# First batch's sketches by rows, features from PSUM on VectorE, and the last group expert by expert in a sketched-attention and expert-attention kernel

## The chip, the cores and the metric

The kernel runs on one core of a Trainium2 chip. The metric is the device time of one execution in microseconds (us), as the median of several runs; lower is better. The engines are TensorE (PE in the profile; PEld is its weight load, which overlaps its matmuls), VectorE (DVE), ScalarE (ACT), GpSimd (POOL) and SyncE (SP), which here only issues transfers. SBUF is the on-chip memory, PSUM the accumulators that matmuls write.

## What is computed

The sizes are B=4 batches, H=4 heads, S=1088 rows, D=32, r=8. The first stage is attention through polynomial sketches, the second a mixture of four attention experts of which each row uses two:

```python
def phi(x):                              # 64 features of a row and head
    a = np.einsum('rd,bhsd->bhsr', S1, x)
    b = np.einsum('rd,bhsd->bhsr', S2, x)
    return np.einsum('bhsi,bhsj->bhsij', a, b).reshape(*x.shape[:-1], r * r)
q_p, k_p = (phi(q), phi(k))
kv = np.einsum('bhsf,bhsd->bhfd', k_p, v)
z = np.sum(k_p, axis=2)
x = np.einsum('bhsf,bhfd->bhsd', q_p, kv) / (np.einsum('bhsf,bhf->bhs', q_p, z)[..., None] + 1e-06)
# (B,H,S,D) -> (B,S,128)
logits = x @ w_gate                      # 4 experts, the 2 largest are kept
w = softmax(the two kept logits)
for e in range(4):
    scores = (x @ wq[e]) @ (x @ wk[e]).T / 8      # causal
    a = softmax(scores)
    out += w_e * ((a @ (x @ wv[e])) @ wo[e])      # w_e is 0 where e isn't kept
```

S1 and S2 come as float64 and are turned into two float32 parts, a high and a low one, by integer work on VectorE ("decode").

## The kernel before, in words

**An order by hand.** The program is a list of numbered jobs (class `Plan`). A job names its engine, or two that could do it, the values that it reads and makes and the buffers that it holds. `ORDER` (L21 to L69) is a list of job numbers; a letter behind a number says which of the two engines takes the job. The jobs are issued in that order, so it fixes the order of the instructions in the queue of each engine; nothing is moved later. An engine takes its instructions in this order and waits where an operand isn't there. Semaphores come from the framework. Jobs are numbered as they are made, so any change of the jobs comes with a new list. The figures in the jobs (`0.153`, `d_us(n)`) are what the maker of the list reckoned with; the program doesn't read them.

**Tiles.** There are four PSUM buffers of two banks each (`pair`). Rows go in 17 tiles of 64, and these in three groups: tiles 0 to 5, 6 to 11, 12 to 16. A score row (68 of them, 17 per batch) is one tile of queries against all keys up to it; its 128 partitions are 64 rows, each with its two chosen experts.

**The first stage, for each batch.** S1 and S2 are loaded (L233) into a buffer that was set to zero (L236) and decoded on VectorE (L302 to L317); `SK` is copied to four groups of partitions (L191). Meanwhile PE runs 8 matmuls of zeros to warm up (L247). k and q are loaded (L423 to L462) and transposed in blocks of 32 on VectorE (`turn k`, `turn q`, L482 to L494). The sketches (L518) are matmuls of 32x32 tiles, 32x288 each: 32 for a tensor and half of the decoded table, once with the high and once with the low part. Their results lie by columns and VectorE transposes them back out of PSUM, two of 128x576 for each of k and q (`back`, L522). Features (L527) are the products of a and b, one of 128x576 per head: those of the first batch by VectorE but for a few on POOL, those of k of the later batches mostly by POOL. k's features are summed against v (L558; 72 matmuls of two halves). For the first batch, q's features are then transposed by PE (L592) and multiplied by the sums (numerators, L615); DVE divides (L622 to L624) and PE turns x (L630). The later batches do q with its columns transposed (L686 to L757).

**The second stage.** The gate's logits (L807), the choice of two (L832 to L848), and masks that go to device memory and back (L892, L897; `md`, `mb`). Queries (L960) are kept by a base copy (L969) and a predicated pick (L973). Each score row is then: scores (L998, PE), mask and row minimum (L1010, DVE, `take`), exponential with its sum (L1026, ACT), `guard`, adding 1e-9 to the sum (L1032 on ACT or L1034 on POOL), reciprocal (L1037, DVE), `weigh`, the product with the reciprocal and the gate (L1041, POOL), a transposition by blocks (L1046, DVE). When a group's rows are done, PE takes its weighted sums of x (L1074, the 32-row tiles `xra`, `xrb`, `xrc` of x that come back from device memory `xd`).

**The end of a group.** The sums of two experts of a row are in one PSUM tile. `keep V` copies them to `agg` (L191, ACT or DVE), `patch V` overwrites rows whose second expert is the other one (L1097, DVE), `spread V` multiplies them by the masks, two experts at a time (L1101, POOL, 128x768 in groups of 384 rows). Where the rows of a group are a multiple of 128, PE multiplies by `Mo` in 128x128 pieces (L1144), piece by piece over the four experts; ACT copies each piece or all (L191) and SP stores (L1157, L1160). The group of 320 rows goes by columns (L1124), is transposed back (L1127) and stored (L1130). In the last batch the groups come in the order second, third, first.

## Time and profile before

| | |
|---|---|
| time, median of 3 runs | 279.67 us (279.2 to 280.02) |
| the profiled execution's own time | 280.91 us |
| its span on the engines | 279.2 us |
| mean granted TensorE clock | 0.994 |
| busy share | PE 94%, PEld 70%, DVE 78%, ACT 36%, POOL 55% |
| DMA | 27.36 MB moved, mean 98 GB/s; HBM read 22.22 MB, written 4.52 MB |

How to read the rows. A line of a view of groups or of the timeline names the source line (L998 is line 998 of the kernel), the engine, the operation, the tile written and the tile or tiles read (out<-in, without buffer numbers), the shapes as partitions x elements with the type, and the count (x216). In the timeline the first two figures are the start in the span and the duration, and the bracket at the end is the idle time ahead of it with what ended it. In the groups the figures behind the bar are the summed busy time, the mean of one in ns, and the idle time of the engine just before. Matmuls are counted in pairs of records where a float32 matmul runs in two passes, so a loop of 64 shows as x128. In the chain of waits, followed back from the last instruction, each step has its start, its length and its line; "issue" is time in which an engine waited for nothing that the profile shows.

### The profile page before, as it was taken

The numbers are of one execution on the slowest core, as the hardware profiler recorded it, in microseconds if no ns is written. First come the engines' busy times: TensorE is split into PE (matmuls) and PEld (weight loads), VectorE is DVE, ScalarE is ACT, GpSimd is POOL, SyncE is SP. The second block draws the span as 40 slices with busy tenths as digits, with TensorE's granted clock in tenths as the row PEclk, the third lists the DMA queues.
The fourth block names the chain that finished last, engine by engine and source line by source line (L and its number), as shares of the span: only waits on it lengthen the run. The fifth ranks groups of instructions, "written<-read, shape, count | busy, mean of one in ns | idle before, by whom it ended". The sixth has DMA issues, their size and how long they took to land.

```text
span 279.2 us, 9471 instructions
## 1 busy us (share of the span) xinstructions
PE 263.8 (94%) x3953; PEld 194.8 (70%) x3953; DVE 218.8 (78%) x541; ACT 100.2 (36%) x272; POOL 153.3 (55%) x246
## 2 busy tenths in 40 slices
PE   5789899899999999989999999999999999999993
PEld 1478575448486796676589976756696975789973
DVE  4895998999989987998969437999898468986340
ACT  2030346254333444433462331463423335233110
POOL 6323636677789834546565458655447432544570
PEclk9979999999999999999999999999999999999999
DMA  8855749921617879243900166701403756820012
GB/s 179 139 141 102 112 124 258 153 34 24 143 32 120 166 184 180 57 102 65 198 6 4 30 150 141 162 2 38 108 2 76 130 116 133 165 56 5 2 31 52
DMA packets 85547, 27.36 MB, mean 98 GB/s; under 512 B 54080, under 2 KB 84864, under 8 KB 85504
## 3 DMA queue, kind: packets, MB, share of 16 engines
q1 hardware_dynamic: 83280, 26.47, 46.4%
q8 instruction: 31, 0.51, 0.8%
q10 hardware_dynamic: 2224, 0.28, 0.6%
q14 instruction: 12, 0.10, 0.1%
HBM read 22.22 MB, written 4.52 MB: 96 GB/s over the span
## 4 chain that ended last, share of the span: by engine, by line
PE 70%; DVE 20%; issue 5%; POOL 2%; ACT 1%; DMA 1%; DVEq 0%; POOLq 0%
PE pair L1074 24%; PE pair L998 19%; PE pair L960 9%; PE pair L1144 6%; PE pair L518 3%; PE pair L558 3%; DVE AT L1046 2%; DVE w L522 2%; DVE w L1010 2%; DVE fp L527 2%; PE pair L1124 2%; PE pair L615 1%; PE pair L592 1%; DVE in L494 1%; DVE xT L191 1%
## 5 line engine op out<-in xcount | busy, mean ns | idle before, releaser
L1041 POOL TENSOR_SCALAR w<-w,rs,sh 128x384 f32<-128x384 f32 (+15 forms) x68 | 55.6, 824 | 54.8 <-DVE rs L1037 52.0
L998 PE MATMUL pair<-xT,qs 128*128 128x384 f32 (+11 forms) x216 | 76.8, 482 | 1.7 <-DVE agg L191 1.3
L1026 ACT ACTIVATE w<-w,mx 128x640 f32<-128x640 f32 (+15 forms) x68 | 52.4, 770 | 72.3 <-DVE mx L1010 56.6
L998 PEld LDWEIGHTS pair<-xT,qs 128*128 128x128 f32 x216 | 37.7, 190 | 26.9 <-issue 10.0
L1046 DVE STREAM_TRANSPOSE AT<-w 128x576 f32<-128x576 f32 (+13 forms) x68 | 50.6, 758 | 5.4 <-POOL w L1041 5.2
L1010 DVE CUSTOM_DVE_ANT_0 w<-pair,mask 128x768 f32<-128x768 f32 (+13 forms) x68 | 48.3, 721 | 5.4 <-PE pair L998 4.7
L1074 PEld LDWEIGHTS pair<-AT,xra 32*128 32x128 f32 x1136 | 41.6, 185 | 6.0 <-DVE mx L1010 2.6
L1074 PE MATMUL pair<-AT,xra 32*128 32x192 f32 (+5 forms) x1136 | 44.5, 303 | 0.0
L1101 POOL TENSOR_TENSOR agg<-agg,mb 128x768 f32<-128x768 f32 (+1 forms) x24 | 37.3, 1565 | 12.7 <-ACT agg L191 6.6
L960 PE MATMUL pair<-xT,Mq 128*128 128x384 f32 (+1 forms) x96 | 34.9, 478 | 0.1
L527 POOL TENSOR_TENSOR fp<-w 128x576 f32<-128x576 f32 x21 | 25.4, 1224 | 14.2 <-DVE w L522 12.5
L191 ACT COPY agg<-pair 128x384 f32<-128x384 f32 (+1 forms) x33 | 14.0, 462 | 44.2 <-PE pair L1074 37.7
L1074 PE MATMUL pair<-AT,xrb 32*128 32x160 f32 (+5 forms) x752 | 26.9, 287 | 0.3 <-issue 0.3
L1074 PEld LDWEIGHTS pair<-AT,xrb 32*128 32x128 f32 x752 | 26.1, 186 | 1.0 <-issue 1.0
L1144 PEld LDWEIGHTS pair<-Mo,agg 128*128 128x128 f32 x192 | 23.4, 192 | 4.1 <-POOL agg L1101 1.7
L1144 PE MATMUL pair<-Mo,agg 128*128 128x128 f32 x192 | 24.9, 279 | 1.0 <-POOL agg L1101 0.9
L960 PEld LDWEIGHTS pair<-xT,Mq 128*128 128x128 f32 x96 | 17.2, 190 | 11.2 <-issue 3.2
L973 DVE COPY_PREDICATED qs<-mb,pair 128x768 f32<-128x768 uint16 (+1 forms) x24 | 23.0, 960 | 2.4 <-DMA mb<-md 1.8
L191 DVE COPY agg<-pair 128x384 f32<-128x384 f32 (+1 forms) x15 | 7.9, 532 | 13.1 <-PE pair L1074 11.7
L518 PE MATMUL pair<-in,SK 32*32 32x288 f32 x416 | 13.4, 494 | 3.0 <-DVE in L494 3.0
L522 DVE STREAM_TRANSPOSE w<-pair 128x576 f32<-128x576 f32 x16 | 11.6, 756 | 5.6 <-PE pair L518 5.6
L1097 DVE COPY_PREDICATED agg<-mb,pair 128x384 f32<-128x384 uint16 (+1 forms) x24 | 12.6, 550 | 3.3 <-ACT agg L191 2.9
(160 smaller groups left out, 295.4 us busy)
## 6 DMA issues: line engine op xcount, KB each, us to landing
mb<-md SPq DMA_DIRECT2D x7, 576.0 KB, 5.2
xra<-xd SPq DMA_DIRECT2D x16, 192.0 KB, 4.3
xrb<-xd SPq DMA_DIRECT2D x16, 192.0 KB, 3.6
xrc<-xd SPq DMA_DIRECT2D x16, 160.0 KB, 4.9
mb<-md SPq DMA_DIRECT2D x4, 480.0 KB, 5.4
in<-in_k_dram SPq DMA_DIRECT2D x12, 136.0 KB, 4.1
in<-in_q_dram SPq DMA_DIRECT2D x3, 544.0 KB, 5.5
xd<-w SPq DMA_DIRECT2D x12, 136.0 KB, 3.5
```

The costliest lines, as they stand in the source:

```text
L191: (nc.scalar.copy if eng == "ACT" else VEC[eng].tensor_copy)(o, i)
L527: VEC[e].tensor_tensor(out=f, in0=a[:, :, None, R : 2 * R].to_broadcast([128, NJ, R, R]), in1=a[:, :, 0:R, None].to_broadcast([128, NJ, R, ...
L960: nc.tensor.matmul(plan[ps[x]][:, y, 0:w], Mq[:, ((1, 2), (0, 3))[x][y]], plan[xT][:, 64 * t0 : 64 * t1], start=True, stop=True)
L973: nc.vector.copy_predicated(chosen(), rows(c), rows(plan[ps[x]]))
L998: nc.tensor.matmul(plan[p][:, y, 0 : c1 - c0], plan[qs][:, 128 * t : 128 * t + 128], plan[xT][:, c0:c1], start=True, stop=True)
L1010: nc.vector.tensor_tensor_reduce(out=o, in0=src, in1=msk, scale=-1.0, scalar=mx[:, b, i, x - 1 : x] if x else 3e38, op0=ALU.add, op1=ALU.m ...
L1026: nc.scalar.activation(out=a, in_=a, func=ACTF.Exp, bias=mx[:, b, i, last : last + 1], scale=-1.0, accum_out=zs[:, b, i : i + 1])
L1041: nc.gpsimd.tensor_scalar(out=a, in0=a, scalar1=rs[:, b, i : i + 1], scalar2=plan[("sh", b)][:, i : i + 1], op0=ALU.mult, op1=ALU.mult)
L1046: nc.vector.transpose(dst[:, 0 : keys // 32, t], plan[A][:, 0:keys].rearrange("p (j s) -> p j s", s=32))
L1074: nc.tensor.matmul(plan[Vk[g // 2]][:, g % 2, lo : 32 * nt], plan[(f"xr{j // 12}", b)][rows, j % 12], a[rows, j, lo:], start=(j == 0), sto ...
L1101: nc.gpsimd.tensor_tensor(out=a, in0=a, in1=plan[mb][:, 2 * x : 2 * x + 2, 0:w], op=ALU.mult)
L1144: nc.tensor.matmul(plan[p][0:m, 0, 128 * x : 128 * x + 128], plan[agg][:, e, 128 * x : 128 * x + m], Mo[:, e], start=(e == 0), stop=(e == ...
```

## The change

- **S loads and decode.** S1 and S2 are each loaded twice, into rows 0 to 15 and 16 to 31, by the queue of SP and that of ACT; the memset of that buffer goes. The decode is in two halves, for the high part and the low part. Besides `SK` it fills block tables `SKW`, which are zero but for each head's own 16 columns.
- **k first.** The first half of the first batch's k goes out first, on ACT's queue.
- **First batch's sketches by rows.** `sketch_rows` takes 64 rows of two heads as the stationary operand and `SKW` as the moving one: 64x64 tiles, 32 columns, 144 matmuls for k and q. The results lie by rows in PSUM. ACT copies the first factor (and the fourth head's second factor) to SBUF; `head_features` multiplies: heads 0 to 2 on VectorE with the second factor read straight from PSUM, head 3 on POOL, in two parts of 4 and 5 blocks of 128 rows (k: 5 and 4). The back transpositions of this batch go. k's sums are in two parts as well, and the features' transpositions of q's first part no longer wait for the second.
- **Second batch's k by rows.** Nine matmuls of 128x128 give the high and the low part beside each other (`sketch_all`), ACT copies them out, POOL adds the two parts (four instructions) and makes the features in five pieces (`row_features`).
- **Reciprocals.** `invert` has a second engine: POOL raises to the power -1. In the new list 32 of the 68 score rows use it.
- **Last group expert by expert.** For the last group of the last batch, VectorE multiplies the first expert of each pair straight out of PSUM by its mask, ACT keeps the second, VectorE patches it and `scale_one` multiplies it by its mask. PE takes the experts in the order 0, 2, 1, 3, three pieces of 128 rows each; ACT or DVE copy each piece, and the three pieces are stored separately, one by SP and two by ACT.
- **A new list.** `ORDER` is another, for 1307 jobs instead of 1270; it also has 20 warming matmuls (18 at the start, 2 among the last group's projections) instead of 12 (8 at the start, 4 at 47 us), and other engines for some jobs. The k of batches 2 and 3 stays as it was, with two back transpositions and four features each.

```diff
--- before
+++ after
@@ ORDER @@
-56 45 47 0 1 8a 77 60 46 3 2 76 25a 19a 17a 48 79 49 51 78 57 90 89 74 87 75 88 50 13b 98 100 99 102a 103a 91 92 83 93
...
+71 0 46 45 85 5a 40b 19b 42a 29a 10a 12b 2 98 1 47 44 51 55 87 52 86 99 89 38a 15a 27a 59 30a 74 8b 88 62 60 33a 54 50
...
     def load_sketch(eng, x):
-        eng.dma_start(out=room(0, 64)[R * x : R * x + R], in_=(S1, S2)[x].bitcast(I32))
-
-    def first():
-        nc.vector.memset(room(0, 64), 0)
+        for r in (R * x, 2 * R + R * x):
+            eng.dma_start(out=room(0, 64)[r : r + R], in_=(S1, S2)[x].bitcast(I32))
...
     def make_ident():
+        nc.gpsimd.memset(SKW, 0.0)
...
+    def decode(lower):
...
+        if not lower:
+            ve.tensor_scalar(out=ex, in0=hi, scalar1=20, scalar2=0x7FF, op0=SHR, op1=AND)
+            ve.tensor_scalar(out=ma, in0=hi, scalar1=0xFFFFF, scalar2=3, op0=AND, op1=SHL)
+            ve.tensor_scalar(out=sg, in0=hi, scalar1=31, scalar2=31, op0=SHR, op1=SHL)
+            ve.tensor_scalar(out=ex, in0=ex, scalar1=896, scalar2=0, op0=ALU.subtract, op1=ALU.max)
+            ve.scalar_tensor_tensor(out=ma, in0=lo, scalar=29, in1=ma, op0=SHR, op1=OR)
+            ve.tensor_single_scalar(ex, ex, 255, op=ALU.min)
+            ve.scalar_tensor_tensor(out=sg, in0=ex, scalar=23, in1=sg, op0=SHL, op1=OR)
+            ve.tensor_tensor(out=ma, in0=ma, in1=sg, op=OR)
+            ve.scalar_tensor_tensor(out=S_hi, in0=ex, scalar=0, in1=ma.bitcast(F32), op0=ALU.is_gt, op1=ALU.mult)
+            ve.transpose(SK[0:32, 0], S_hi)
+        else:
+            ve.tensor_single_scalar(lw, lo, 0x1FFFFFFF, op=AND)
+            ve.tensor_copy(last, lw)
+            ve.scalar_tensor_tensor(out=S_lo, in0=last, scalar=2.0**-52, in1=sg.bitcast(F32), op0=ALU.mult, op1=ALU.mult)
+            ve.transpose(SK[0:32, 1], S_lo)
+    def spread_blocks(e, h, s):
+        copy(e, SKW[32 * h : 32 * h + 32, s, :, h, :], SK[0:32, s, 0 : 2 * R].rearrange("d (x r) -> d x r", x=2))
...
-            job(f"load k{b}.{x}", "SP", 0.45 if early else 0.7, lambda e, x=x: load_k(nc.sync, x), lead,
-                ("kin", b, x if early else 0), [kin], landing=1.6 if early else 0.95, rank=rank(-0.1))
+            job(f"load k{b}.{x}", ("ACT", "SP")[x] if early else "SP", 0.45 if early else 0.7,
+                lambda e, x=x: load_k(nc.scalar if e == "ACT" else nc.sync, x), lead,
...
+        def sketch_rows(nm, j0, j1, t):
+            src = plan[("in", nm + "T", b)]
+            for j in range(j0, j1):
+                for m in range(2):
+                    for half in (0, 64):
+                        rows, y = slice(64 * m, 64 * m + 64), 128 * j + half
+                        for s in range(2):
+                            nc.tensor.matmul(plan[t][half : half + 64, m, 32 * (j - j0) : 32 * (j - j0) + 32].rearrange(
+                                "p (x d) -> p x d", x=2), src[rows, y : y + 64],
+                                SKW[rows, s, :, 2 * m : 2 * m + 2].rearrange("p x h r -> p x (h r)"),
+                                start=(s == 0), stop=(s == 1))
+        def kept_first(nm, j0, j1):
+            return plan[ab[nm]][:, 4 * R * j0 : 4 * R * j1].rearrange("p (m j d) -> p m j d", m=2, d=2 * R)
+        def kept_last(nm, j0, j1):
+            return plan[ab[nm]][:, 4 * R * NJ + R * j0 : 4 * R * NJ + R * j1].rearrange("p (j r) -> p j r", r=R)
+        def in_psum(t, nj):
+            return plan[t][:, :, 0 : 4 * R * nj].rearrange("p m (j x d) -> p m j x d", x=2, d=2 * R)
+        def copy_sketch(y, nm, j0, j1, t):
+            s = in_psum(t, j1 - j0)
+            if y == 0:
+                for m in range(2):
+                    nc.scalar.copy(kept_first(nm, j0, j1)[:, m], s[:, m, :, 0])
+            else:
+                nc.scalar.copy(kept_last(nm, j0, j1), s[:, 1, :, 1, R:])
+        def head_features(e, nm, h, j0, j1, t):
+            nj = j1 - j0
+            r = slice(R * (h % 2), R * (h % 2) + R)
+            second = in_psum(t, nj)[:, h // 2, :, 1, r] if h < 3 else kept_last(nm, j0, j1)
+            f = plan[fps[nm]].rearrange("p (j h x y) -> p j h x y", h=H, x=R, y=R)[:, j0:j1, h]
+            VEC[e].tensor_tensor(out=f, in0=second[:, :, None, :].to_broadcast([128, nj, R, R]),
+                                 in1=kept_first(nm, j0, j1)[:, h // 2, :, r, None].to_broadcast([128, nj, R, R]), op=ALU.mult)
+        def sketch_all(nm, j0, j1, t):
+            src = plan[("in", nm + "T", b)]
+            for j in range(j0, j1):
+                nc.tensor.matmul(plan[t][:, (j - j0) // 4, 128 * (j % 4) : 128 * (j % 4) + 128], src[:, 128 * j : 128 * j + 128],
+                                 SKW.rearrange("p s x h r -> p (s x h r)"), start=True, stop=True)
+        def sketch_keep(nm, a, j0, j1, t):
+            src = plan[t][:, a, 0 : 128 * (j1 - j0)].rearrange("p (j y d) -> p y j d", y=4, d=4 * R)
+            nc.scalar.copy(plan[ab[nm]].rearrange("p (y j d) -> p y j d", y=4, j=NJ)[:, :, j0:j1], src)
+        def sketch_add(nm, j0, j1):
+            a = rows_ab(nm)
+            for x in range(2):
+                nc.gpsimd.tensor_tensor(out=a[:, 0, x, j0:j1], in0=a[:, 0, x, j0:j1], in1=a[:, 1, x, j0:j1], op=ALU.add)
+        def row_features(e, nm, j0, j1):
+            a = rows_ab(nm)[:, 0, :, j0:j1].rearrange("p x j (h r) -> p x (j h) r", h=H)
+            n = H * (j1 - j0)
+            f = plan[fps[nm]].rearrange("p (j h x y) -> p (j h) x y", h=H, x=R, y=R)[:, H * j0 : H * j1]
+            VEC[e].tensor_tensor(out=f, in0=a[:, 1, :, None, :].to_broadcast([128, n, R, R]),
+                                 in1=a[:, 0, :, :, None].to_broadcast([128, n, R, R]), op=ALU.mult)
...
+        tcuts = ((0, 4), (4, NJ))
+        kcuts = ((0, 5), (5, NJ))
...
+                    for h in range(H):
+                        n = R * R * nj
+                        job(f"{'phi' if h < 3 else 'features'} {nm}{b}.{h}{x}", "DVE" if h < 3 else "POOL", d_us(n) - 0.05 if h < 3 else 0.09 + 0.0019 * n,
+                            lambda e, nm=nm, h=h, j0=j0, j1=j1, t=t: head_features(e, nm, h, j0, j1, t),
+                            [("ab", nm, b, x, 0)] + ([("ab", nm, b, x, 1)] if h == 3 else []), ("fp", nm, b, x), [*([t] if h < 3 else []), ab[nm], fps[nm]], rank=at + 0.01 * h)
...
+            elif b == 1 and nm == "k":
...
-        def invert():
-            nc.vector.reciprocal(rs[:, b, i : i + 1], rs[:, b, i : i + 1])
+        def invert(e):
+            r = rs[:, b, i : i + 1]
+            if e == "DVE":
+                nc.vector.reciprocal(r, r)
+            else:
+                nc.gpsimd.tensor_tensor(out=r, in0=r, in1=minus, op=ALU.pow)
...
-        job(f"invert {b}.{i}", "DVE", 0.153, lambda e: invert(), [("zg", b, i)], ("r", b, i), rank=rank)
+        job(f"invert {b}.{i}", ("DVE", "POOL"), (0.153, 0.555), invert, [("zg", b, i)], ("r", b, i), rank=rank)
...
+        if last_group(b, n):
+            def mix(x):
+                nc.vector.tensor_tensor(out=by_half(plan[agg][:, x]), in0=sums_of(x), in1=by_half(plan[mb][:, x]), op=ALU.mult)
+            def scale_one(e, x):
+                a = plan[agg][:, 2 + x, 0:w]
+                VEC[e].tensor_tensor(out=a, in0=a, in1=plan[mb][:, 2 + x, 0:w], op=ALU.mult)
...
+            def project_expert(e, first_, last_):
+                for x in range(3):
+                    nc.tensor.matmul(piece(x), plan[agg][:, e, 128 * x : 128 * x + 128], Mo[:, e], start=first_, stop=last_)
+            def keep_piece(e, x):
+                copy(e, plan[ob][:, 128 * x : 128 * x + 128], piece(x))
+            def store_piece(e, x):
+                (nc.scalar if e == "ACT" else nc.sync).dma_start(out=out[b, 64 * t0 + 128 * x : 64 * t0 + 128 * x + 128],
+                                                                in_=plan[ob][:, 128 * x : 128 * x + 128])
+            order = (0, 2, 1, 3)
+                job(f"out {b}.{n}.{e}", "PE", 12 * 0.056, lambda _, e=e, y=y: project_expert(e, y == 0, y == 3),
...
```

## The prediction

> **What bounds the kernel now.** I read the page first, then the busy time by stage, then the timeline of the head and of the end, then the chain of waits. The page:
>
> ```profile
> PE 263.8 (94%) x3953; PEld 194.8 (70%) x3953; DVE 218.8 (78%) x541; ACT 100.2 (36%) x272; POOL 153.3 (55%) x246
> PE 70%; DVE 20%; issue 5%; POOL 2%; ACT 1%; DMA 1%; DVEq 0%; POOLq 0%
> ```
>
> TensorE looks saturated, but 94% is an average over stages. The busy time of each engine in stretches that I cut at the events named below (columns: stretch, its length, busy time of PE, PEld, DVE, ACT and POOL with instructions, granted clock, DMA share, GB/s), and of DVE alone from the first division to the last transposition ahead of the first group's sums:
>
> ```profile
> 16.30:19.80 3.50, 3.50 (x28) 3.17 (x30) 3.50 (x6) 1.44 (x4) 0.00 (x0) 0.51 0.71 191
> 23.10:62.90 39.80, 36.77 (x463) 23.39 (x459) 37.24 (x107) 16.74 (x49) 23.33 (x50) 1.00 0.71 137
> 62.90:178.00 115.10, 113.69 (x1785) 85.37 (x1784) 95.20 (x230) 43.35 (x122) 72.33 (x104) 1.00 0.51 103
> 178.00:268.90 90.90, 90.54 (x1390) 71.58 (x1390) 68.20 (x162) 34.26 (x90) 45.12 (x61) 1.00 0.34 71
> 268.90:279.20 10.30, 5.51 (x32) 4.14 (x32) 2.60 (x5) 1.34 (x3) 3.28 (x2) 1.00 0.16 35
> ...
> 24.75:60.89 36.14, 33.79 (x99) 1.00 0.76 146
> ```
>
> So there are three stages. To 23 us PE waits for the first batch's sketches and features. From 23 to 63 us DVE is busy 37.24 of 39.80 us. From 63 us on PE is busy 98.8% (113.69 of 115.10), then 99.6% (90.54 of 90.90). After 268.9 us comes a tail of 10.30 us with PE busy about half. A change pays in the first two stages and in the tail; in the third only what TensorE itself does counts. The chain of waits confirms the second stage; in its middle it runs through DVE:
>
> ```profile
> 47.54 1.50 DVE fp L527
> ...
> 49.39 1.29 DVE fp L735
> 50.68 0.93 DVE qs L973
> ```
>
> The head (start, duration, engine, line, operation, tiles, shapes, count):
>
> ```profile
> 1.31 3.59 PE L247 MATMUL pair<-idle 128*128 128x512 bf16 x8 [1.31 <-DVE idle L240]
> 3.79 0.58 DVE L302 TENSOR_SCALAR w<-w 32x32 int32<-32x32 int32 x1 [2.54 <-DMA w<-in_S_dram]
> 7.93 4.95 PE L518 MATMUL pair<-in,SK 32*32 32x288 f32 x128 [3.03 <-DVE in L494]
> 12.04 2.82 DVE L527 TENSOR_TENSOR fp<-w 128x576 f32<-128x576 f32 x2
> ...
> 16.26 2.77 DVE L527 TENSOR_TENSOR fp<-w 128x576 f32<-128x576 f32 x4
> 16.28 2.79 PE L592 MATMUL pair<-ident,fp 128*128 128x128 f32 x12 [0.23 <-DVE w L522]
> 19.00 2.62 PE L558 MATMUL pair<-vp,fp 128*64 128x33 f32 x72
> 21.55 1.60 PE L518 MATMUL pair<-in,SK 32*32 32x288 f32 x64
> 23.09 4.23 PE L615 MATMUL pair<-kvz,fp 128*128 128x66 f32 x36
> 24.75 0.17 DVE L622 TENSOR_SCALAR den<-pair 128x12 f32<-128x12 f32 x1
> 27.96 2.31 POOL L527 TENSOR_TENSOR fp<-w 128x576 f32<-128x576 f32 x2 [1.49 <-DVE den L622]
> 28.14 0.56 DVE L624 TENSOR_TENSOR w<-pair,den 128x384 f32<-128x384 f32 x1
> 30.22 1.46 POOL L370 CAST AT<-ident 64x1536 bf16<-64x1536 f32 x1
> 30.23 1.48 DVE L833 TENSOR_TENSOR ch<-ch 128x12 f32<-128x12 f32 x1
> ...
> 60.52 0.45 DVE L1046 STREAM_TRANSPOSE AT<-w 128x256 f32<-128x256 f32 x1
> 62.89 0.61 PE L1074 MATMUL pair<-AT,xra 32*128 32x192 f32 x8
> ```
>
> Two things to see. The same 64 sketch matmuls took 4.95/2 = 2.5 us at 7.93 and 1.60 us at 21.55, and the clock was granted at 0.51 from 16.3 to 19.8. And a DVE feature product took 1.41 us (2.82/2) beside POOL's, 0.69 us (2.77/4) alone, while L624, one of whose inputs is PSUM, took 0.56 us beside POOL's L527.
>
> **The change part by part.** Prices of single instructions, by shape (count, busy, mean ns, idle before), and the landing of a k load (us to landing last):
>
> ```profile
> L522 DVE STREAM_TRANSPOSE w<-pair 128x576 f32<-128x576 f32 x16 | 11.6, 756 | 5.6 <-PE pair L518 5.6
> L1037 DVE RECIPROCAL rs<-rs 128x1 f32<-128x1 f32 x68 | 8.9, 140 | 7.8 <-POOL rs L1034 5.9 <-ACT rs L1032 1.7
> L1097 DVE COPY_PREDICATED agg<-mb,pair 128x384 f32<-128x384 uint16 x16 | 8.8, 579 | 0.7 <-ACT agg L191 0.4
> ...
> L867 POOL TENSOR_TENSOR ch<-ch,c 128x44 f32<-128x44 f32 x1 | 0.7, 687 | 0.1
> L340 POOL TENSOR_TENSOR pick<-pick 128x8 f32<-128x8 f32 x1 | 0.2, 203 | 0.1
> ...
> in<-in_k_dram SPq DMA_DIRECT2D x1, 256.0 KB, 4.0
> ```
>
> *Start of the sketches.* k's first half goes first on ACT's queue, so it is in by about 0.8 + 4.0 = 4.8 us at the latest. But S1 and S2 are each loaded twice now, two issues a queue, S2 behind k; the decode, which starts at 3.79 in the old kernel, stands behind those issues and behind two transpositions of k on DVE, say at 5. From decode to sketches the old kernel took 7.93 - 3.79 = 4.1 us for 16 instructions, a copy and q's transpositions; the new one has 14, three k transpositions and four block copies, about as much. POOL's one-hot cast (1.46 us) now falls on the decode's second half; L833 waited through it. So first sketches at 8.7 to 11, taken 9.5, against 7.93: +1.6. k first buys nothing by itself.
>
> *Sketches by rows.* 144 matmuls, seen as 288, replace 128 for k and q of the first batch; tiles of 64x64 are not in the trace. Below: 4.6 us, if four tiles overlap where L558's two do not (half of 2.62/72 = 36 ns is 18; 16 ns taken). Above: 288 x 36 ns = 10.4. I take 25 ns, as L518 (1.60/64): 7.2 us, to 16.7. The old pair took 4.95. The 18 instead of 8 warming matmuls (3.59/8 = 0.45 us each) last to about 9, so the clock should be full here and in the transpositions L592, which took 2.79/12 = 0.23 us at 0.51.
>
> A rule of the Trainium skill speaks against this step: "TensorE: Matmul & The Clock Gate" (Wait — 56ns, not 53.3ns?) says that with hardware decode off the sequencer spends about 62 ns on each matmul; by it 288 of them would take 17.9 us, an estimate from the page, and the forecast would come out about 10 us later. L518's 25 ns (1.60/64) do not agree, so that floor is not in force here.
>
> *Features.* Four back transpositions of 0.756 us leave DVE (3.0). Twelve products of 256 or 320 columns read PSUM: by L624 (0.56 us for 384) 0.40 to 0.48 each, 5.3 in all, where six of 576 took 2.82 + 2.77 = 5.6. Twelve small ACT copies come ahead of them. DVE's order puts the first product of q's second part ahead of k's second part, so nearly six products follow q's last sketch: 16.7 + 0.6 + 2.6 = 19.9. Then k's sums (2.62, at most), eight transpositions (0.9 to 1.9), the second batch's sketches by nine matmuls of 128 columns (18 records at 2.50/20 = 0.125, a row of the tail below: 2.3) stand ahead of the numerators: 24.3, against 23.09. Term: **+1.2**, from -1.6 to +4.
>
> The products are priced as unhindered. The Trainium skill, "GPSIMD Engine Reference" (Specifications), names contention with DVE instructions of two SBUF inputs; the 1.41 us of two-SBUF-input products beside POOL and the 0.56 us of L624 beside it agree; were PSUM no shelter, twelve products at double price would add 5 us.
>
> *DVE from the first division to the last transposition of the first group.* 33.79 us of work in 36.14. From the order of the new instructions, with the old durations, that stretch loses two of three 576-wide products (2.05, one of them the slow one), one back transposition of the second batch's k (0.7; k's features go to POOL), a turn of q (0.6), L833's stall (1.0 with its neighbours, the one-hot cast being early), one score and one pick that now come later (1.5); a few copies come. 28.0 us remain; at the same density (93%) 30.0. That is -6.1; PE's own queue shares it, so I take **-5.5**, from -3.0 (all that PE idles in 23.1:62.9, 39.80 - 36.77) to -7.
>
> *Thirty-two of 68 reciprocals become a power on POOL.* DVE loses 32 x 0.14 = 4.5 us and waits that stood behind it; POOL gains 32 x 0.2 (L340) to 0.69 (L867), taken 0.4: 13 us. No row shows a power. In the third stage DVE has 20 us to spare to 178 us and POOL 43, so both are cover; without it, each power adds its price less 0.14 to the way exp, weigh, turn, sums. With the new order and copies moved to ACT: **-1.0**, from -4 to +5, since PE lacks only 1.8 us in that stage by the records.
>
> *Tail.* Old rows:
>
> ```profile
> 268.78 2.42 PE L1124 MATMUL pair<-agg,Mo 128*128 128x320 f32 x8
> 268.92 0.86 ACT L191 COPY agg<-pair 128x384 f32<-128x384 f32 x2 [2.66 <-PE pair L1074]
> 269.61 3.30 POOL L1101 TENSOR_TENSOR agg<-agg,mb 128x768 f32<-128x768 f32 x2 [1.88 <-ACT agg L191]
> ...
> 272.96 2.50 PE L1144 MATMUL pair<-Mo,agg 128*128 128x128 f32 x20 [0.95 <-POOL agg L1101]
> 275.54 0.48 ACT L191 COPY ob<-pair 128x384 f32<-128x384 f32 x1 [5.76 <-issue]
> 276.04 0.39 SPq L1157 DMA_DIRECT2D out_dram<-ob  x1
> ```
>
> From the last sum to the end: 10.3. New, counted from there: DVE multiplies one expert (0.58) and patches two (0.58 each) by 1.8; then its queue holds the turn of the other group's output, which waits for PE's L1124 until 2.4, and ends at 2.9; second expert 3.5, last scaling 4.1; POOL's one scaling (half of 1.65) is done long before. PE's last six matmuls end at 4.9, ACT's two copies at 5.5, its two stores are issued by 6.3 (0.39 each), and land 2.8 later as before (279.2 - 276.43): 9.1. **-1.3**, from -2.4 (no wait in DVE's queue) to -0.4.
>
> Sum: 1.2 - 5.5 - 1.0 - 1.3 = -6.6. The profiled execution took 280.91 us (span 279.2), 1.2 over the median of 279.67; I put the difference on the median: **273.1 us**.
>
> **Rivals.**
> - *Sketches eat the head.* At 36 ns, with a start at 11, the numerators begin 4 us later than now: 273.1 + 2.8 = 276. For it: 288 tiny matmuls; against: L518's 25 ns with two tiles fewer in conflict.
> - *PE is already the bound in the second stage.* Then only its 3.0 us of idle can go there, and -1.0 becomes 0: 273.1 + 2.5 + 1.0 = 276.6. For it: 36.77 of 39.80 busy; against: ends of matmuls are modelled, and the chain above runs on DVE.
> - *Slower: the power on POOL.* Place: between guard and weigh of 32 of 68 score rows, in POOL's queue, with the spreads of the sums behind it. Each costs its price less 0.14 where POOL is the late one; if that is one time in two, 6.6 us are gone at 0.14 + 6.6/16 = 0.55 us a power, and at 1.0 us it is 273.1 + 16 x 0.6 = 283. For it: no row has this operation, and L867 needs 0.69 for 44 elements; against: 0.20 for eight elements, and POOL idles 45%.
> - *More than forecast.* DVE off the path up to 178 us and a short sketch: -1.6 - 7 - 2.5 - 1.4 = -12.5: 267.
>
> **How the numbers follow.** Forecast 0.52, sketches 0.13, PE bound 0.11, power 0.15, more 0.09. About 0.3% (0.8 us) can be told from no change. Faster: 0.52 + 0.09 + 0.20 of the two middle rivals' 0.24 = 0.81; slower 0.13 + 0.02 = 0.15; same 0.04. The range 267.5 to 279.5 leaves out the slow power case (0.15) and a little below.
>
> **What would show it.** First matmul on SKW near 9.5 us and 25 ns between them; granted clock 1.00 all through 9 to 24; numerators near 24; first weighted sum near 58 instead of 62.89; POOL's power near 0.4 us; the tail 9 us with the turn of the output ahead of the second expert's product. Wrong, if the first sums start after 61, if PE idles more than 2% between them and the tail, or if powers take over 0.6 us.

## The result, and the profile after

The changed kernel takes 281.36 us (median of 17 runs, 280.08 to 288.46) against 279.90 us before (17 runs beside them): a ratio of 1.0065, 95% interval 1.0039 to 1.0091, so 1.8 us slower where 6.6 us faster was forecast. In part of the runs of most kernels with the changed head the granted clock is 0.98 or 0.97 and the time 2 to 7 us longer; the ratios leave the longest of these out. The profiled execution took 281.35 us (span 279.6).

The page of the changed kernel, busy time and the chain's shares by engine:

```profile
PE 265.6 (95%) x4074; PEld 198.4 (71%) x4075; DVE 211.2 (76%) x519; ACT 105.1 (38%) x288; POOL 169.9 (61%) x286
PE 75%; DVE 6%; DMA 6%; issue 4%; POOL 3%; ACT 2%; SPq 1%; DVEq 0%; POOLq 0%; ACTq 0%
```

DVE does 7.6 us less than before and has gone from 20% to 6% of the chain, as was meant. The time did not follow. The view by stages shows why (columns as in the prediction; the cuts are the first numerators, the first weighted sums and the end of the last ones; first the changed kernel, then the same cut of the old one):

```profile
0.00:23.34 23.34, 19.14 (x414) 13.95 (x415) 14.63 (x46) 6.23 (x22) 11.83 (x41) 1.00 0.73 147
23.34:60.78 37.44, 35.83 (x457) 23.12 (x456) 32.13 (x99) 16.39 (x50) 28.13 (x58) 1.00 0.89 154
60.78:270.05 209.27, 205.19 (x3174) 157.00 (x3173) 161.23 (x368) 81.21 (x214) 129.06 (x186) 1.00 0.43 85
270.05:279.60 9.55, 5.39 (x33) 4.31 (x34) 3.22 (x7) 1.29 (x4) 0.92 (x1) 1.00 0.19 40
```

```profile
0.00:23.09 23.09, 17.25 (x293) 10.34 (x293) 15.56 (x39) 4.46 (x9) 9.27 (x30) 0.93 0.66 139
23.09:62.90 39.81, 36.78 (x463) 23.41 (x459) 37.24 (x107) 16.74 (x49) 23.33 (x50) 1.00 0.71 137
62.90:268.90 206.00, 204.23 (x3174) 156.95 (x3174) 163.39 (x391) 77.62 (x211) 117.45 (x165) 1.00 0.43 89
```

From the numerators to the end PE is busy for 265.55 - 19.14 = 246.4 us now, and was for 263.77 - 17.25 = 246.5 (the sums of the two views less their first rows). The second stage is 2.4 us shorter, but 0.95 us of this is PE work that now stands behind the first sums, and PE's idle time there fell only from 3.03 to 1.61. In the third stage it rose from 1.77 to 4.08; three waits make 2.9 of that (0.96 us for features on POOL at 112 us, 1.26 us behind no semaphore at 150 us, 0.72 us for a copy on ACT at 170 us). The tail lost 0.75 us.

The head of the changed kernel (start, duration, engine, line, operation, tiles, shapes, count, idle before):

```profile
1.24 6.95 PE L254 MATMUL pair<-idle 128*128 128x512 bf16 x18 [1.24 <-DVE idle L243]
6.48 1.49 POOL L386 CAST AT<-ident 64x1536 bf16<-64x1536 f32 x1
6.68 1.33 DVE L324 SCALAR_TENSOR_TENSOR w<-w 32x32 f32<-32x32 f32 x1
8.12 0.30 PE L571 MATMUL pair<-SKW,in 64*64 64x32 f32 x2
9.23 0.42 PE L571 MATMUL pair<-SKW,in 64*64 64x32 f32 x6 [0.81 <-DVE SKW L193]
9.99 3.35 PE L571 MATMUL pair<-SKW,in 64*64 64x32 f32 x196 [0.34 <-ACT SKW L193]
14.45 1.58 PE L571 MATMUL pair<-SKW,in 64*64 64x32 f32 x84 [1.12 <-issue]
15.96 1.09 PE L718 MATMUL pair<-ident,fp 128*128 128x128 f32 x8
23.34 2.79 PE L741 MATMUL pair<-kvz,fp 128*128 128x66 f32 x24
```

A sketch matmul takes 3.35/196 = 17 ns, not 25. The sketches begin in earnest at 9.23 (9.5 was taken), numerators at 23.34, not 24.3. In the middle stands an idle time of 1.12 us behind no semaphore ("issue"); more on it in the last section. The decode's L324 waited through the one-hot cast, as expected.

The groups of the products and of the powers (count, busy, mean ns, idle before):

```profile
L599 DVE TENSOR_TENSOR fp<-pair,w 128x320 f32<-128x320 f32 x6 | 2.7, 484 | 2.1 <-ACT w L590 2.1
L599 DVE TENSOR_TENSOR fp<-pair,w 128x256 f32<-128x256 f32 x6 | 2.3, 414 | 0.0
...
L1167 POOL TENSOR_TENSOR rs<-rs,minus 128x1 f32<-128x1 f32 x32 | 18.0, 562 | 12.0 <-ACT rs L1158 7.8 <-DVE qs L1099 3.1
```

The products that read PSUM cost what was estimated (0.40 to 0.48). A power costs 0.562 us, not 0.4.

The tail of the changed kernel:

```profile
266.86 3.18 PE L1204 MATMUL pair<-AT,xra 32*128 32x192 f32 x92
269.97 2.42 PE L1275 MATMUL pair<-agg,Mo 128*128 128x320 f32 x8
272.22 2.84 PE L1301 MATMUL pair<-Mo,agg 128*128 128x128 f32 x24
272.43 0.52 DVE L1278 STREAM_TRANSPOSE ob<-pair 128x320 f32<-128x320 f32 x1 [0.29 <-PE pair L1275]
275.39 0.36 SPq L1307 DMA_DIRECT2D out_dram<-ob  x1
275.56 0.85 ACTq L1307 DMA_DIRECT2D out_dram<-ob  x2
```

The new projection's matmuls follow the other group's on PE without a gap, where PE waited for POOL's spreads before. The last stores are issued by 276.41, 6.4 us behind the last sum (forecast 6.3), and took 3.2 us to the end, not 2.8.

### The profile page after: what moved, and what is told of

It reads as the page before. It is cut to its first block, busy times and chain, and to the rows that moved or that the text cites. A ratio compares the mean times of both kernels' runs of the same rounds, so it can differ in the third digit from the quotient of the medians.

```text
span 279.6 us, 9762 instructions
## 1 busy us (share of the span) xinstructions
PE 265.6 (95%) x4074; PEld 198.4 (71%) x4075; DVE 211.2 (76%) x519; ACT 105.1 (38%) x288; POOL 169.9 (61%) x286
## 4 chain that ended last, share of the span: by engine, by line
PE 75%; DVE 6%; DMA 6%; issue 4%; POOL 3%; ACT 2%; SPq 1%; DVEq 0%; POOLq 0%; ACTq 0%
PE pair L1204 23%; PE pair L1124 21%; PE pair L1086 8%; PE pair L1325 6%; PE pair L677 3%; PE pair L1275 3%; PE pair L535 2%; PE pair L571 2%; DMA vp<-in_v_dram 2%; DMA xd<-w 2%; PE pair L741 1%; DMA out_dram<-ob 1%; POOL agg L1231 1%; DVE w L1136 1%; PE pair L933 1%
## 5 line engine op out<-in xcount | busy, mean ns | idle before, releaser
L1152 ACT ACTIVATE w<-w,mx 128x128 f32<-128x128 f32 (+14 forms) x68 | 52.4, 770 | 64.5 <-DVE mx L1136 52.4
L1171 POOL TENSOR_SCALAR w<-w,rs,sh 128x512 f32<-128x512 f32 (+15 forms) x68 | 55.6, 822 | 19.3 <-DVE rs L1165 15.6
L1136 DVE CUSTOM_DVE_ANT_0 w<-pair,mask 128x768 f32<-128x768 f32 (+14 forms) x68 | 48.3, 727 | 11.4 <-PE pair L1124 11.1
L1176 DVE STREAM_TRANSPOSE AT<-w 128x512 f32<-128x512 f32 (+16 forms) x68 | 50.3, 757 | 3.8 <-POOL w L1171 3.7
L1204 PE MATMUL pair<-AT,xra 32*128 32x160 f32 (+5 forms) x1136 | 44.8, 302 | 0.0
L1204 PEld LDWEIGHTS pair<-AT,xrb 32*128 32x128 f32 x752 | 26.7, 185 | 1.5 <-issue 1.5
L1167 POOL TENSOR_TENSOR rs<-rs,minus 128x1 f32<-128x1 f32 x32 | 18.0, 562 | 12.0 <-ACT rs L1158 7.8
L1325 PEld LDWEIGHTS pair<-Mo,agg 128*128 128x128 f32 x168 | 19.9, 192 | 2.2 <-issue 0.8
L1160 POOL TENSOR_SCALAR rs<-zs 128x1 f32<-128x1 f32 x29 | 7.0, 243 | 23.5 <-ACT w L1152 15.2
L1325 PE MATMUL pair<-Mo,agg 128*128 128x128 f32 x168 | 20.6, 276 | 0.0
L544 POOL TENSOR_TENSOR fp<-w 128x576 f32<-128x576 f32 x13 | 15.3, 1176 | 0.2
L193 ACT COPY qs<-pair 128x384 f32<-128x384 f32 (+1 forms) x22 | 9.4, 470 | 15.7 <-PE pair L1086 8.4
```

Source lines behind the costliest of these rows:

```text
L193: (nc.scalar.copy if eng == "ACT" else VEC[eng].tensor_copy)(o, i)
L1136: nc.vector.tensor_tensor_reduce(out=o, in0=src, in1=msk, scale=-1.0, scalar=mx[:, b, i, x - 1 : x] if x else 3e38, op0=ALU.add, op1=ALU.m ...
L1152: nc.scalar.activation(out=a, in_=a, func=ACTF.Exp, bias=mx[:, b, i, last : last + 1], scale=-1.0, accum_out=zs[:, b, i : i + 1])
L1167: nc.gpsimd.tensor_tensor(out=r, in0=r, in1=minus, op=ALU.pow)
L1171: nc.gpsimd.tensor_scalar(out=a, in0=a, scalar1=rs[:, b, i : i + 1], scalar2=plan[("sh", b)][:, i : i + 1], op0=ALU.mult, op1=ALU.mult)
L1176: nc.vector.transpose(dst[:, 0 : keys // 32, t], plan[A][:, 0:keys].rearrange("p (j s) -> p j s", s=32))
```

## The experiments

Ratios are to the kernel before on the same chip, with 95% intervals; 0.36% is 1 us. Where only the list is edited, the diff names the jobs.

### The parts alone

Powers undone in the changed kernel:

```diff
-invert 0.1@POOL ... (32 rows)
+invert 0.1@DVE ... (32 rows)
```

> The changed kernel with all 68 reciprocals on DVE again (the 32 powers on POOL took 0.562 us each, 18.0 us in all). Theory A: the powers are what gave the third stage its new idle time of PE (4.1 us from the first sums to the tail, 1.8 in the old kernel): PE's idle there falls to about 2 us, the time by 1.5 to 2.5 us against the changed kernel, to about 279. Theory B: the new order of the jobs is what made it, and the powers lie in time that POOL has to spare: idle stays at 3.5 to 4.5 us and the time within 0.7 us of the changed kernel's 281.4, more likely above it, since DVE gets 32 x 0.14 us back.

Measured: 294.54 us, 1.0516 (1.0465 to 1.0567). Neither theory: it is 13 us slower than the changed kernel, and tells of something else. The group of the reciprocals in that kernel:

```profile
L1165 DVE RECIPROCAL rs<-rs 128x1 f32<-128x1 f32 x68 | 8.9, 147 | 11.6 <-ACT rs L1158 6.8 <-POOL rs L1160 4.8
```

The instruction costs 0.147 us, but DVE now stands idle for 11.6 us ahead of these, waiting for `guard`, with minima and transpositions queued behind. The 32 places in the list suit POOL's queue and not DVE's, so the run says nothing of the power's price. The clean form is the next one, which puts the powers into the kernel before:

```diff
-invert 0.1@DVE ... (the same 32 rows)
+invert 0.1@POOL ...
```

> The kernel before with the same 32 reciprocals as powers on POOL, nothing else. Theory A: POOL gets 18 us more, sums wait for weighed rows, PE's idle time in the third stage goes from 1.8 to about 4 us: 1.5 to 2.5 us slower than before. Theory B: POOL has the room: within 0.7 us of before. My forecast took -1.0 for this step with the order and copies; by it the run is 0 to 1 us faster.

Measured: 281.47 us, 1.0043 (1.0025 to 1.0061), +1.2 us, between the theories and on the slower side. The powers' group in this kernel:

```profile
L1044 POOL TENSOR_TENSOR rs<-rs,minus 128x1 f32<-128x1 f32 x32 | 18.6, 581 | 9.7 <-ACT rs L1035 8.6
```

Each costs 0.44 us more than DVE's reciprocal (0.581 - 0.14). 1.2 us is what some three of the 32 would cost if they lay on the path to the sums (an estimate, 1.2/0.44; which of them do was not traced).

The last group, undone in the changed kernel and alone in the old one:

```diff
 def last_group(b, n):
-    return b == B - 1 and n == 0
+    return False
```

> The changed kernel with the last group's end as in the old one (four copies, two patches, two spreads on POOL, pieces one by one, one store). The tail after the last weighted sum was 10.3 us before and 9.55 after. If the tail was worth what these spans say, this is 0.75 us slower than the changed kernel with a tail of 10.3; by my forecast 1.3 slower; if the end of the changed kernel is set elsewhere (stores of the other group), no change.

Measured: 281.99 us, 1.0069 (1.0035 to 1.0103). It is slower than the changed kernel's 1.0065 by too little to be told from nothing; the intervals allow 0.75 us, and 1.3 us only just. So this run doesn't show that the new end is worth anything in the changed kernel.

```diff
+if last_group(b, n): mix, keep, patch, scale; project_expert; store_piece
```

> The kernel before with the last group's end of the changed one, nothing else. By the spans 0.75 us faster than before (tail 9.55), by my forecast 1.3 us (tail 9.0); if the gain in the changed kernel came from the other order of the last rows, about 0.

Measured: 278.97 us, 0.9950 (0.9930 to 0.9970): 1.4 us faster. The stretch behind the last sum in this kernel:

```profile
268.63:277.30 8.67, 5.03 (x33) 4.21 (x32) 3.24 (x7) 1.29 (x4) 0.92 (x1) 0.93 0.19 42
```

8.67 us, where the forecast had 9.1 and the old kernel 10.30. In the old kernel this step was right. By its ratio this kernel is the fastest of all that were run, ahead of the kernel before and of the changed one; the next ones (0.9971, 0.9977) overlap with it.

The changed head alone, with the old order from the numerators on, and then with the second batch's k by rows:

```diff
-            elif b == 1 and nm == "k":
+            elif False:
```

> The changed kernel's head alone (k first, decode in halves, first batch's sketches by rows, features from PSUM, 18 warming matmuls), then the old order to the end, the second batch's k, the reciprocals and the last group as before. By the spans of the two profiles numerators start at 23.3 instead of 23.1, and what DVE saves behind them buys nothing if PE is the bound: 0 to 0.7 us slower than before. By my forecast (+1.2 for the head, about -2 for the stall and the turn of q that go from DVE's stretch): 0.5 to 1 us faster.

Measured: 280.88 us, 1.0041 (1.0012 to 1.0070): 1.15 us slower, outside both readings. In its profile numerators begin at 25.24, 2.15 us later than before, and the stretch from there to the first sums is 38.60 us, 1.2 us shorter. In three of the twelve runs the granted clock was 0.97 or 0.982 and the time 283.0 to 284.5 us; the median of the other nine is 280.5, 0.5 us above before, so part of the 1.15 us is the clock.

> As the run with the head alone, and the second batch's k by rows too (nine matmuls of 128x128, copies on ACT, adds and five feature pieces on POOL): two back transpositions (1.4 us) and one product (1.4 us) less on DVE, about 3 us more on POOL. By my forecast about 2 us faster than the head alone; if PE is the bound, within 0.7 us of it; if POOL's pieces come late for the sums against v, up to 1.5 us slower.

Measured: 280.92 us, 1.0054 (1.0022 to 1.0087). Taking three DVE instructions of the second batch away on top of the head brings nothing that can be told from the head alone.

### What bounds the second stage

```diff
-            job(f"pick {b}.{n}.{x}", "DVE", d_us(2 * w), lambda _, x=x: pick(x),
+            job(f"pick {b}.{n}.{x}", "DVE", d_us(2 * w), lambda _, x=x: None if b == 0 else pick(x),
```

> The kernel before without the six predicated picks of the first batch (its queries stay those that the base copies wrote): DVE does about 6 x 0.97 = 5.8 us less before the first group's sums, nothing else changes for PE. If DVE bounds the second stage, as the step -5.5 of my forecast has it, the time falls by about 5 us, to 275. If PE bounds it, only PE's idle time of that stage (3.0 us) can go: 0.5 to 2.5 us faster.

Measured: 279.94 us, 1.0001 (0.9984 to 1.0017). This is the run that settles the largest term. The second and third stage of this kernel, cut at the same events as above:

```profile
22.27:62.19 39.92, 36.55 (x462) 23.38 (x457) 32.01 (x101) 16.74 (x49) 23.36 (x50) 1.00 0.74 137
62.19:267.25 205.06, 203.44 (x3174) 156.54 (x3173) 163.43 (x390) 77.61 (x211) 117.44 (x165) 1.00 0.43 89
```

DVE has 32.01 us of work where it had 37.24, and the stretch is as long as before (39.92 against 39.81), with PE at 36.55. 5.2 us of DVE are worth nothing. PE's two longest waits in this stage are the same (in us: total, times, longest), first in the kernel before, then in this one:

```profile
PE pair L906 <- DVE ch L811: 1.4, 1, 1.4
PE pair L757 <- DVE w L522: 0.9, 1, 0.9
```

```profile
PE pair L757 <- DVE w L522: 1.6, 1, 1.6
PE pair L906 <- DVE ch L811: 1.4, 1, 1.4
```

They are for two single results of DVE, the choice of experts and one back transposition, and neither wait got shorter with less work elsewhere in DVE's queue.

The opposite, more work for PE:

```diff
-dummy22@- dummy19@- dummy26@- dummy7@-
+score 0.4.00 dummy22@PE ... score 0.2.00 dummy19@PE ... query 0.2.01 dummy26@PE ... query 0.2.11 dummy7@PE
```

> The kernel before with eight more warming matmuls (0.39 us each, 3.1 us of PE) spread over 35 to 57 us, behind four jobs of scores and queries. If PE bounds the second stage: 2 to 3.1 us slower. If DVE bounds it, PE has 3.0 us to spare there and the time moves by less than 1 us.

Measured: 281.41 us, 1.0054 (1.0033 to 1.0074): +1.5 us for 3.1 us of matmuls, between the two readings. PE had room for half of them. So neither engine's busy time alone gives the length of the stage: PE's work does for the most part, with about 1.5 us of waits in it that more work can use.

### The order

```diff
 ORDER: the changed kernel's jobs (abridged)
-the changed kernel's order and engines behind the numerators
+the old kernel's order and engines behind the numerators, where it has the job
```

The list of jobs also says which engine takes a job, and some 75 jobs differ in this between the two lists (`guard`, copies and features above all). What this run tells apart is the list as a whole, not the order alone.

> All parts of the change (head, second batch's k by rows, 32 powers on POOL, last group expert by expert), but behind the numerators in the old order. The parts alone gave: head with k by rows +1.5 us (0.54%), powers +1.2, last group -1.4. If they add, this is 1.3 us slower than before, where the changed kernel is (+1.8): then the new order is worth about nothing. If the new order is what costs, this is within 0.5 us of before; if the new order makes room for the powers on POOL, this is over 2.5 us slower than before.

Measured: ratio 0.9996 (0.9963 to 1.0029); median of all runs 280.76. All parts of the change, by the old list, take what the old kernel takes. The second stage, the third and the tail of this kernel, cut at the same events:

```profile
23.07:62.31 39.24, 36.54 (x458) 23.32 (x457) 33.08 (x100) 17.84 (x54) 25.21 (x53) 1.00 0.69 134
62.31:268.63 206.32, 204.24 (x3174) 156.78 (x3173) 162.68 (x363) 77.90 (x213) 134.22 (x195) 1.00 0.43 89
268.63:277.17 8.54, 5.03 (x33) 4.21 (x32) 3.24 (x7) 1.29 (x4) 0.91 (x1) 1.00 0.19 42
```

PE idles 2.1 us in the long third stretch (206.32 - 204.24), against 4.1 in the changed kernel, although POOL has the powers here too (134.22 us). Ahead of the first sums it is the other way round: 2.70 us here, 1.61 in the changed kernel. So the new list wins 1.1 us of idle time in the second stage and loses 2.0 in the third; its tail is 1.0 us longer in these two profiles. The parts alone sum to 1.5 + 1.2 - 1.4 = 1.3 us; the interval of this run, -1.0 to +0.8, misses that, but with the parts' own intervals (together about 1.2 us either way) the two agree.

The same without the powers (68 reciprocals on DVE):

> All parts of the change but the powers (68 reciprocals on DVE), in the old order. The powers cost 1.2 us when put into the kernel before. If they cost the same here, this is 1.2 us faster than all parts in the old order, about 1.2 under before; if the head and the last group leave POOL the room, within 0.4 us of it.

Measured: 0.9977 (0.9942 to 1.0013), median 280.80. The two intervals overlap too far to say what the powers cost here.

Two picks behind three transpositions, in the changed kernel:

```diff
-pick 2.0.0@DVE pick 2.0.1@DVE weigh 1.12 turn A 1.12 ... turn A 1.14 ... turn A 1.13
+turn A 1.14 turn A 1.13 weigh 1.12 turn A 1.12 pick 2.0.0@DVE pick 2.0.1@DVE
```

> The changed kernel with two picks of the third batch put behind three transpositions (turn A) in DVE's order. In the changed kernel they waited 1.0 us for a mask fetch at 146.7 us, with the transpositions behind them, and PE idled 1.26 us at 149.7. If that idle time hangs on DVE's queue, it goes: 1.2 us faster than the changed kernel, and fewer runs at a low clock. The view of waits says "issue" there, that is no semaphore; if PE ran out of instructions (its last instruction packet came at 148.2 and took 1.36 us), the gap stays at 149 to 151 us and the time within 0.5 us of the changed kernel.

Measured: 281.04 us, 1.0039 (1.0007 to 1.0071). PE's gap stayed at 150.1 us with 1.00 us, so it doesn't hang on DVE's queue. The changed kernel's waits at that place:

```profile
PEld pair L1204 <- issue: 1.5, 1, 1.5
PE pair L1204 <- issue: 1.3, 1, 1.3
```

### Filling idle times of PE

In the old kernel with the new last group; then there without the move at 32 us and with a fuller one at 124 us (copies on ACT, a transposition of x later); then that one with all parts by the old list:

```diff
-widen 1@PE widen 0@PE query 0.0.00@PE
+query 0.0.00@PE widen 1@PE widen 0@PE
-choose a2.0 choose b2.0 ... patch V 1.0.0 ... patch V 1.0.1 ... keep V 1.0.1@DVE
+choose a2.0 patch V 1.0.0 patch V 1.0.1 keep V 1.0.1@DVE choose b2.0
```

> The kernel before with the changed last group and three jobs moved in the order: the first batch's second query matmul ahead of the mask matmuls that wait for the choice (PE idle 1.37 us at 32.4), and the patches and one copy of the second batch's first sums ahead of the second half of the third batch's choice on DVE (PE idle 1.32 us at 124.3, score waiting for a PSUM buffer). If PE's idle time is what counts everywhere: 1.4 (last group) + 0.9 + 1.3 = 3.6 us faster than before. If a stall filled in one place comes back in the next: 1.4 us faster, as the last group alone.

Measured: 279.78 us, 0.9997 (0.9980 to 1.0014): slower than the same kernel without the filling (0.9950). The score that waited at 124.3 starts at once, and the next pair of scores waits instead, in this kernel's timeline:

```profile
126.78 1.29 DVE L770 STREAM_TRANSPOSE w<-xT 128x1088 f32<-128x1088 f32 x1
128.23 0.73 DVE L1011 CUSTOM_DVE_ANT_0 w<-pair,mask 128x576 f32<-128x576 f32 x1
129.02 2.29 PE L999 MATMUL pair<-xT,qs 128*128 128x352 f32 x4 [1.83 <-DVE mx L1011]
```

In this profile the granted clock is 0.50 from 129.50 to 132.91, right behind that gap (more in the last section).

> The kernel before with the changed last group and the same filling (the other filling, of the idle time at 32 us, left out). If the idle time at 124 us goes without one in its place: 1.4 + 1.3 = 2.7 us faster than before, 277.3. If it comes back further on, as in the run with both fillings, 0 to 1.4 us faster.

Measured: 278.96 us, 0.9971 (0.9953 to 0.9990): no better than the last group alone; the gap stands at 127.9 with 1.59 us.

> All parts of the change in the old order, and one idle time of PE (1.32 us at 124.3, a score that waits for a PSUM buffer) filled: four copies on ACT and two patches ahead of the second half of the choice on DVE, a transposition of x behind the score's minimum. Of 12 runs without this, seven took 278.9 to 279.4 us and five 282.2 to 283.5, nearly all of those at a clock of 0.982. If idle times over about 1.3 us bring a window of 3.41 us at half clock (1.7 us), the low clocks go and the median falls from 280.8 to 278 to 278.5. If the low clocks have another cause, about half the runs stay at 282 to 283.

Measured: 279.41 us, 0.9980 (0.9963 to 0.9997), with the gap come back at 133 us in the same way. One run of twelve had a clock of 0.982 instead of five, but its profile shows the low clock in the head (last section), which the filling doesn't touch, and full clock behind the gap at 133 us: the first reading falls. That fewer runs had it is not explained by this.

### Warming

```diff
-9 jobs of two warming matmuls at the start
+4 jobs
```

The kernel before has eight at the start too; of its other four, two come at 12.8 us and two at 47.7.

> The changed kernel with 8 warming matmuls at the start instead of 18 (they end at about 4.5 us, the first sketch starts at 8.1). If the long warming is what lowers the granted clock later, the time falls by 0.5 to 1 us and the clock is above 0.985 in all runs. If it is needed for the sketches, they run at half the clock as in the old kernel (16.3 to 19.8 us) and the time rises by 1 to 3 us.

Measured: 283.50 us, 1.0119 (1.0077 to 1.0160): 2.1 us slower than the changed kernel, with clocks of 0.980 to 0.992. In its profile two stretches behind 3.41 us with PE nearly idle are at half clock, and the sketches fall into them:

```profile
5.58:8.99 3.41, 0.28 (x2) 0.19 (x2) 3.10 (x11) 0.46 (x1) 1.87 (x3) 1.00 1.17 220
8.99:12.40 3.41, 2.86 (x89) 2.75 (x91) 1.99 (x8) 1.13 (x3) 0.00 (x0) 0.50 0.46 97
12.40:15.82 3.42, 3.42 (x139) 3.42 (x137) 2.33 (x7) 0.87 (x6) 1.99 (x4) 0.50 0.81 126
```

> The kernel with the changed head alone, 8 warming matmuls instead of 18. Same two readings: 0.5 to 1 us faster than the head alone (+1.15 us against before) if the long warming lowers the clock later, 1 to 3 us slower than it if the sketches need it.

Measured: 281.05 us, 1.0026 (1.0009 to 1.0043). The shorter warming makes the changed kernel slower, and its profile shows the second reading at work; that the long warming lowers the clock later is not borne out. The head alone comes out no slower with the shorter one, and its profile has full clock in the sketches: the warming is not needed in every execution.

Ten more matmuls of zeros in the head:

```diff
+dummy, dummy ahead of sketch k0.0
             if nm == "k" and j0:
+                for _ in range(6):
+                    nc.tensor.matmul(plan[t][:, 0, 256:512], idle[:, 0:128], idle[:, 0:256], start=True, stop=True)
```

> All parts of the change but the powers, in the old order, and ten more short matmuls of zeros where PE idles in the head: four of 512 columns ahead of the first sketch, six of 256 columns behind k's second sketch. In the profile with the low clock of the run with the filled order the clock was 0.50 from 16.27 to 26.51 us, right behind a stretch of 3.41 us in which PE was busy for 1.88; the numerators began at 27.5 instead of 23.3. If such idle time in the head is what lowers the clock, no run of this is above 280 and the median is 277.5 to 278.2 (280.8 without these matmuls, the five fastest of 12 at 277.5 to 278.1), the fastest of all versions. If the clock falls by itself, a third to a half of the runs stay at 281 to 284.

Measured: 279.22 us, 0.9980 (0.9960 to 1.0001), one run of twelve at a clock of 0.982. The low clock nearly went, as the first reading has it, but the median stays a full 1.0 us above what that reading gave.

> The changed kernel with the same ten matmuls. If idle time in its head lowers the clock in part of its runs, the runs over 282.5 us (6 of 17 without them) go and the median falls to 280 to 280.8; what is left above before (0.1 to 0.3%) is the new order's and the powers'. If not, the median stays at 281.4 or above.

Measured: 282.15 us, 1.0088 (1.0061 to 1.0115), every run at a clock of 0.994 or more. With the clock all but full throughout, the changed kernel is still as slow: what it lost is not the clock.

## Why the prediction was wrong, step by step

- **"DVE from the first division to the last transposition of the first group": -5.5, wrong, and the step that failed.** I took a stretch in which DVE is busy 93% for one that DVE bounds, and let its length shrink with DVE's work. The row beside it had PE at 36.77 of 39.80. Taking 5.2 us from DVE there left the stage as long (39.92 against 39.81 us) and moved the time by 0.0 (0.9984 to 1.0017); PE's two long waits in it, for single results of DVE, stayed. I had the bound of 3.0 us from PE's idle time at hand, used it only as the near end of the term's range, and gave the rival "PE is already the bound" 0.11. That rival named the right engine, though its 3.0 us, all of PE's idle time, were too much as well. The first sums came 2.1 us sooner in the changed kernel (60.78, where the prediction had near 58), but the third stage was 3.3 us longer: 0.96 us of it PE's work, moved from ahead of the sums, and 2.3 us more idle time.
- **The new list, within the -5.5 and the -1.0: taken as a gain, a loss of about 1.9 us.** I had no row for it, and let the moved rows count in DVE's favour. The same jobs by the old list are at 0.9996, by the new one at 1.0065; the intervals leave 0.8 to 3.1 us. The view by stages has 2.0 us more of PE's idle time in the third stage, 1.1 us less in the second, and a longer tail. Whether the order or the choice of engines does it was not tried.
- **"Thirty-two of 68 reciprocals become a power on POOL": -1.0, wrong in sign.** +1.2 us alone. The price is 0.562 us, not 0.4, and above the break-even of 0.55 that the rival named; but by the estimate above it decided about one time in ten, not one in two: the rival had the sign right and the size too large.
- **"Sketches by rows", "Features" and their term of +1.2: near in size by luck.** The items that the prediction sets ahead of the numerators, 2.62, 0.9 to 1.9 and 2.3 us behind 19.9, give 25.7 to 26.7, not its 24.3, unless part of them overlaps, which it doesn't say. The sketches ran at 17 ns instead of 25 and the products as priced, and in the changed kernel the numerators came only 0.25 us later. The head alone costs 1.15 us, but with numerators 2.15 us later, a shorter second stage and part of the runs at a low clock; "the clock should be full here" didn't hold in all runs.
- **"Tail": -1.3, right in the old kernel.** -1.4 us alone, 8.67 us where 9.1 was worked out. In the changed kernel the tail was 9.55 us, 0.75 less than before, and undoing the step there moved the time by nothing that can be told.
- **The second batch's k by rows**, in the -5.5 with about 2.7 us of DVE work: worth nothing that the runs show (1.0041 and 1.0054 without and with it).

None of the three signs that the prediction set for being wrong came true, all by a little: the first sums started at 60.78 (61 was set), PE idled 1.95% of the third stage (2%), a power took 0.562 us (0.6). They were set too far out to catch a change that is slower.

The part that was priced step by step along PE's waits, the tail, came out right; the parts that were priced by an engine's busy time did not. What stays open: which waits of the new list cost most, and what the head costs. The longest wait, at 149.7 us, follows PE's count of instructions (below), and where it was gone (the changed kernel with ten more matmuls) the time was no shorter.

## What to carry to other kernels

Two engines can both look busy in a stretch. Subtract each one's busy time from its length, and before taking work from one of them, let the gain be no larger than what the other idles; then see which single results that other one waits for, since here less work on DVE shortened neither of PE's waits for it. Price a new list of jobs as a risk and not as a free carrier of the gains: put the parts into the old one first, one at a time. The one part here that clearly paid when it was put in alone is the end of the kernel, where the engines wait for each other in turn.

## What the runs showed of the hardware that was not expected

**PE stands still at a fixed count of instructions.** The idle time at 13.3 us in the changed kernel's head stands behind its 222nd matmul record (18 + 2 + 6 + 196, the rows above). With ten more matmuls in the head it comes behind the 222nd again, now in the midst of a tensor's sketches, in the timeline of all parts without the powers and with the warming:

```profile
1.24 7.65 PE L254 MATMUL pair<-idle 128*128 128x512 bf16 x22 [1.24 <-DVE idle L243]
8.82 0.81 PE L571 MATMUL pair<-SKW,in 64*64 64x32 f32 x8
9.97 3.06 PE L571 MATMUL pair<-SKW,in 64*64 64x32 f32 x192 [0.34 <-ACT SKW L193]
14.42 0.43 PE L571 MATMUL pair<-SKW,in 64*64 64x32 f32 x8 [1.39 <-issue]
```

22 + 8 + 192 = 222: the place follows the number of instructions and not the work, which speaks against a buffer or a semaphore. Counted with the weight loads and the waits it is the 449th record of PE, and the gap at 149.7 us comes behind the 4,545th, 4,096 later, in the changed kernel, in the one with the old end, in the one with the moved picks and in the one with eight warming matmuls, 1.00 to 2.29 us long. In the last three a gap of 0.53 to 0.96 us also stands behind the 2,497th, just half way. That PE ran out of instructions is the likely reading; no run changed their supply. PE's instruction queue moved 32 packets in the changed kernel, 0.52 MB, some 16 KB each. The Trainium skill ("Runtime: NRT & Kernel Launch", Instruction fetch mechanics) says that instructions come in blocks of 16 KiB, 256 of them, and that issue is slower than the fetch, which hides it. The sizes agree with the trace; the hiding, by this reading, does not, where 196 matmuls and their loads go in 3.35 us. The 2,048 instructions from one of these three places to the next are what the same section gives for what PE holds; that the one comes of the other was not tried.

**The clock falls for 3.41 us at a time, and can stay low.** The run of all parts by the old list with the filling was profiled with a low clock; its head in stretches of that length (the column before the DMA share is the clock):

```profile
9.44:12.86 3.42, 3.08 (x198) 2.97 (x196) 2.35 (x6) 1.38 (x9) 0.82 (x2) 1.00 0.56 103
12.86:16.27 3.41, 1.88 (x102) 1.74 (x94) 2.50 (x5) 0.33 (x2) 1.72 (x3) 1.00 0.83 123
16.27:19.68 3.41, 3.41 (x38) 3.08 (x38) 2.82 (x7) 1.71 (x6) 2.56 (x8) 0.50 0.82 229
19.68:23.10 3.42, 3.42 (x51) 3.25 (x50) 2.11 (x4) 0.21 (x1) 0.43 (x3) 0.50 0.06 17
23.10:26.51 3.41, 3.41 (x18) 3.41 (x17) 0.00 (x0) 1.38 (x3) 0.00 (x0) 0.50 1.06 150
```

Behind a stretch with PE busy for 1.88 of 3.41 us the clock is 0.50 for three such stretches, though PE is busy throughout; numerators began at 27.54. The Trainium skill ("TensorE: Matmul & The Clock Gate", Part 1: The HAM clock gate) has windows of about 3.4 us that run free of the kernel, half the clock behind an idle one, and full clock again behind one busy one. The length agrees; here a window that was half idle was enough, and three busy ones passed at half the clock. The other profiles bear out the first. In the windows of all twenty profiles the clock went from full to half 28 times, each time behind a window with PE busy for 2.08 us or less; in twelve more such windows (1.62 to 2.07 us) it stayed full. The edges of the windows lie elsewhere in each execution, and in the changed kernel's profile the idle time of the head is split between two, neither of them with less than 2.6 us of work, and the clock stays full:

```profile
10.55:13.96 3.41, 2.79 (x174) 2.67 (x167) 3.33 (x8) 0.87 (x6) 1.94 (x4) 1.00 0.47 82
13.96:17.37 3.41, 2.60 (x92) 2.34 (x93) 1.32 (x5) 1.58 (x8) 1.33 (x3) 1.00 0.95 153
```

So where the edges fall is a likely reason why some runs have the low clock and others don't; no run shows it alone. With the idle time in the head partly filled, it came once in 19 runs of two kernels.

**Small matmuls on quarters of the array overlap.** 17 ns from one 64x64 matmul of 32 columns to the next (3.35 us for 196), with four places in the array in turn; the profile shows each as some 0.22 us long.
